# A new order of turns for a gated recurrence and its MLP on one core

## The chip, the core and the metric

The kernel runs on one core of a Trainium2 chip. The metric is the device time of one execution in microseconds (us); it is measured in several runs, and the median is given. A separate execution is recorded by the hardware profiler; from it come the profile page and the trace, a record of every instruction with its start and duration, of the semaphores, and of the single packets that the DMA queues move.

The engines have short names here as in the profile: PE is TensorE (matmul), PEld its weight loads, DVE VectorE, ACT ScalarE, POOL GpSimd, SP SyncE, which issues nearly all transfers. L765 is line 765 of the kernel.

## What is computed

Four sequences (batch b) of 768 steps, 8 heads of 48 channels. A gated linear recurrence runs along each head, and its outputs, joined to rows of 384, go through a layer norm and an MLP of width 1536:

```python
for t in range(S):                                   # S = 768
    state = alpha[:, :, t, :, None] * state + einsum('bhd,bhe->bhde', k[:, :, t], v[:, :, t])
    y[:, :, t] = einsum('bhd,bhde->bhe', q[:, :, t], state)
x = y.transpose(0, 2, 1, 3).reshape(B, S, H * D)     # 4 x 768 x 384
mu, var = mean(x), mean((x - mu) ** 2)               # along each row
xn = (x - mu) / sqrt(var + 1e-06) * g_ln
out = x + maximum(xn @ w_ch1, 0.0) @ w_ch2           # 384 -> 1536 -> 384
```

The two weight matrices come as 8-byte floats; all else is fp32.

## The kernel before, in words

**Chunks.** The 768 steps are cut into six chunks c of 128. The recurrence of one chunk and one sequence is done with matmuls: within a chunk the products of the gates are taken by logarithms, a triangular matmul (L284, L288: `lps`) and exponentials; q and k are scaled by them (L294, L296), transposed on TensorE (L321: `tps`), multiplied with each other (L337, L345: `aps`), masked (L350, L355), and multiplied with v (L397, L407: `yps`) beside the state that comes in. The new state is k times v (L371: `ups`) with the gates (L380 to L386). The gates of a chunk's end go through DRAM (`row`, L301, and `gate`, L361), to turn rows into columns. Chunk 0 takes 128 steps whole, the others as two halves of 64. The result x is stored to DRAM (`kept`, L426), normalized and transposed (L446: `xps`) into `xT`.

**The MLP.** Chunk 0 takes the two products plainly: L476 is xn times w_ch1 (`hps`), L488 the hidden layer times w_ch2 (`ops`). For chunks 1 to 5 all four sequences are done together by a fast matrix scheme: blocks of x and of the weights are added and subtracted first (`combine_x`, `combine_first`, `combine_hidden`, `combine_weights`), then 15 block products per pair of column blocks (L765) and 20 block products (L588) are taken, and each is added into its results by VectorE, ScalarE and GpSimd (L771 to L808, L598 to L648).

**Transfers.** Inputs of a chunk come by SyncE for two sequences at a time: alpha, k, q (`ra`, `rk`, `rq`, L128; later chunks one sequence at a time, L159), v (`vn`, L134, and half of it again with halves swapped, `vx`, L144). The weights come in 12 pieces of 768 KB (`ws`, L192), six of w_ch1 first, into three staging buffers; VectorE and ScalarE turn each into fp32 (L204 to L214), and the end of one lets the load of the third next start. x comes back from DRAM as the start of the result (`ob`, L463) and the results leave by L467.

**What sets the order.** Each part of the work is a Python generator that emits a few instructions and yields. The string `ORDER` (L25) names, letter by letter, whose turn is next, and the loop at L848 takes one step of that generator:

```python
turns = {"YZ"[h]: first_of_chunk_0(h) for h in range(2)}
turns |= {"PQ"[h]: second_of_chunk_0(h) for h in range(2)}
turns |= {chr(ord("a") + n): attention(n // B, n % B) for n in range(NCB * B)}
turns |= {chr(ord("A") + i): take_weights(i) for i in range(len(pieces))}
...
    for turn in ORDER:
        next(turns[turn], None)
```

So a to x are the recurrence of the 24 pairs of chunk and sequence, A to L the weight pieces, Y and Z the first product of chunk 0, P and Q its second, S and W the combined weights, X and N the combined blocks of x and of the hidden layer, M the block products of chunks 1 to 5, V the first block products of the last chunk, R the ReLUs, O the loads of `ob`. No scheduler moves anything afterwards: every engine's queue, SyncE's too, holds its instructions in the order of the string, and a waiting instruction holds up all behind it on its engine. Buffers rotate in the same order: eight PSUM banks, eleven of `sum` and so on. A letter whose generator has ended does nothing.

Of the kernel before, what the change touches and what calls it, by code (L numbers as in the profile page):

```python
# [22 lines left out]


ORDER = (  # L25
    "aaaabbaaddaacbbbbccccaaababbbccdddaaabbbbfeaAfffeeeadaaebbfdaaddceadcccceeeehAdd"
    "gdAccaachbeAgbfbbffffghddddbcggghccibceeeaggghaeebbifffggfBdddddfjcifggeeecAeeCB"
    "hccefiifhhhhcBBYYYdjhiffcjcdYiiYjjZffZiiYYDjDCBDflCCZZZDkYZZZlhhlihhgiiigjjjilYY"
    "gjgghEYYlGEZZGZhEZYlmkhkjggjghllYYYCkkkGEZhlFFHkkiiiYOOFFFlYYenZZZmlhjjYfHHggDjj"
    "GlmjjkeZZZZYhhhSJZYnkkkleekkkkiOlZnkiemmllYZZiinmmmnnfmmYIeIfholHPPSSomjjSSSkSSm"  # L30
    "KIIkkjKKpjJJnnknQfflQoojLLngggmLWWWQPPSPPSSPPpoSoEnhmmgghhnXQXXOXppQppiiiXXQQSSS"
    "mmmnliOjjXXXSmmlnniijMSoWWWoMMrXMMXooMMMMMMmnnnMMMMMRMMmMmMMqMppMMMMMppWMqolorrp"
    "lpppQjjpRRRMMMMMMMpprppMqqqrLnooqqppqqWWWoMMMMRmrMtRMoMMMMRMMMMMMMnnnMMOMMOssqqO"
    "tqsqskMoRooqqtttqWWRNNNMMMMMRRqtNMNNNnnnnNMMMMMMMMMMMlllMkkkMMMkRNNlNNMMNBtvmWtt"
    "pMMNtrllmMMMMrkkrNNMMMMMMMMMossXXXMMtrvvrrrqqqrrXXXooXMMMMMMMXXMMMoXMXrooMMMMMoM"
    "MsMIMMMMsMrMvssvMMMMvtruuustMssrrrtsssuqmMttMMMMRMMMMtMMtuurrrrMMrMppMMMMMMMqROR"
    "MRRRMMMMRRROMpMMMpNOONNNnMMnMMMMRRRNMMMMMNNNMNMMwNMNMMMMMMMMMMMNNNvvMNNvppovxMoM"
    "MMMmMsMMMxqqqvtAXXsssXXvvvXMXvXvttMuMMMMMXXsXuMMMMMMMMMMMuMMMMRMMOtuXMMxMMMMttMM"
    "MMwwwwuquusvuuMMMMMwwwwMMMxuRMMRRRxMMMMMwMRMMRMMMMMMxxxxMMMOOxRMwswwwvRwxuxNNswx"
    "xxNNKquMMMvvttsuuxMMsMMMtRRNNNMMMRMMMxqNNxNwxrrMMMCMMMNMMMONMMNssMMMNMMMMMMvvvww"  # L40
    "vNNMMMwwtXXXXxXxxXMLuuXXMMMXXMMMMMMMMMMMMMMMMMMwMOuMMwxOxxMMvXuuwMMRMMMMMMMMMMMw"
    "JJMMwMMMMMMRRRMMMMMuMRMMMMMvxRRRMMMRMMMMXXXXVXXXOMMXXXRMMRNMMMMMVVNNVVVVVVVNXNMV"
    "VVVRVVVVVMVVVVVVVVVVNRRMNNVVVVVVVVVVVVMRRRRMMMMMVVVVONNNNNMMMMMMNVRVVVVVMMMMMMVV"
    "VRRVVVVRNRNVVOMMNNMMMNGNNMMMMMMNNMMOOKMMMMMMMMMMMNNNRMMMMMMNNNOMMMMHNMMNMMMMMNMM"
    "MMMMMMMM"
)


# [830 lines left out]
```

## Time and profile before

| | |
|---|---|
| median of 3 runs | 437.04 us (436.31 to 439.61) |
| span of the profiled execution | 437.4 us |
| PE busy | 425.6 us, 97%, 4760 rows |
| PEld busy | 379.7 us, 87%, 4760 rows |
| DVE busy | 342.7 us, 78% |
| ACT busy | 202.4 us, 46% |
| POOL busy | 155.3 us, 36% |
| moved by DMA | 45.52 MB, 104 GB/s in the mean |

The profiler gives no time of its execution other than the span, from the first instruction of the kernel to its last. Shares are of the span. "Busy" of TensorE counts overlapping rows once; its matmuls are pipelined, so the distance from one start to the next tells more than the duration of a row. A wait is shown with the engine and line that ended it, by the semaphore that came last; "issue" is a wait for which the profile shows no semaphore. Transfers are counted by queue: queue 1 holds SyncE's, the queues called "instruction" bring the program itself to the engines.

### The profile page before, as it was taken

To read this page: it belongs to the slowest core of one execution; us is meant where nothing else is said; L and a number is where in the kernel's file an instruction comes from. 1 tells how busy PE (TensorE), PEld (TensorE's weight loads), DVE (VectorE), ACT (ScalarE), POOL (GpSimd) and SP (SyncE) were. 2 spreads that over 40 slices of the span, in tenths; PEclk is the share of its full clock that TensorE was granted. 3 is DMA by queue.
4 is the path that set the end of the run, shared out by engine and by line. 5 is a ranking of instruction groups with operands and counts; after the bars stand their busy time and mean duration, and the time that the engine had idled before them with its cause. 6 is when DMAs were issued, how large, how long until landed. Compare 5 with 4: busy or idle time off the path is not lost.

```text
span 437.4 us, 11604 instructions
## 1 busy us (share of the span) xinstructions
PE 425.6 (97%) x4760; PEld 379.7 (87%) x4760; DVE 342.7 (78%) x654; ACT 202.4 (46%) x499; POOL 155.3 (36%) x164
## 2 busy tenths in 40 slices
PE   7996999999999999999999999999999999999996
PEld 5886888875668889998889998889998899999996
DVE  3997899899899789957778776678676579886783
ACT  5694656743535655634274151665256452312000
POOL 1011041220015644052845152663035571628313
PEclk9999999999999999999999999999999999999999
DMA  8979888755063076023342013300033000001201
GB/s 273 325 200 296 272 228 240 186 164 146 37 184 72 21 206 175 6 84 83 58 131 69 18 39 126 59 20 3 1 109 108 1 1 2 0 0 55 90 20 54
DMA packets 54972, 45.52 MB, mean 104 GB/s; under 512 B 26204, under 2 KB 51036, under 8 KB 54920
## 3 DMA queue, kind: packets, MB, share of 16 engines
q1 hardware_dynamic: 54376, 44.63, 34.8%
q8 instruction: 37, 0.61, 0.6%
q10 hardware_dynamic: 544, 0.17, 0.2%
q14 instruction: 15, 0.12, 0.1%
HBM read 35.25 MB, written 9.53 MB: 102 GB/s over the span
## 4 chain that ended last, share of the span: by engine, by line
PE 79%; DVE 9%; DMA 6%; ACT 4%; issue 1%; POOL 0%; SPq 0%; POOLq 0%; DVEq 0%; ACTq 0%
PE ops L588 30%; PE hps L765 29%; PE ops L488 5%; DMA ws<-in_moe_w_ch_dram 3%; PE yps L407 3%; PE aps L345 3%; PE tps L321 2%; PE xps L446 2%; PE hps L476 2%; DVE w L206 2%; PE ups L371 1%; DMA ra<-in_alpha_dram 1%; DMA gate<-row 1%; DVE ws L212 1%; DVE ws L208 1%
## 5 line engine op out<-in xcount | busy, mean ns | idle before, releaser
L604 POOL TENSOR_TENSOR ob<-ob,u 128x192 f32<-128x192 f32 x40 | 25.9, 658 | 81.0 <-DVE ob L601 61.6
L765 PE MATMUL hps<-sum,w 128*128 128x256 f32 x192 | 47.2, 379 | 0.0
L588 PE MATMUL ops<-w,hT 128*128 128x192 f32 x224 | 40.4, 327 | 0.0
L765 PEld LDWEIGHTS hps<-sum,w 128*128 128x128 f32 x192 | 35.9, 190 | 4.6
L386 POOL TENSOR_TENSOR mid<-mid,gate 112x192 f32<-112x192 f32 x20 | 14.6, 732 | 69.0 <-DVE mid L384 55.3
L816 ACT ACTIVATE hT<-hT 128x512 f32<-128x512 f32 x48 | 28.1, 630 | 21.6 <-POOL hT L787 13.2
L588 PEld LDWEIGHTS ops<-w,hT 128*128 128x128 f32 x224 | 37.1, 190 | 0.5
L476 PE MATMUL hps<-xT,w 128*128 128x256 f32 x144 | 32.6, 380 | 2.9 <-DVE qk L294 2.9
L765 PE MATMUL hps<-xT,w 128*128 128x256 f32 x136 | 34.6, 381 | 0.0
L476 PEld LDWEIGHTS hps<-xT,w 128*128 128x128 f32 x144 | 26.7, 190 | 6.4 <-issue 3.0
L488 PE MATMUL ops<-w,hT 128*128 128x384 f32 x96 | 31.7, 487 | 0.0
L588 PE MATMUL ops<-ws,sum 128*128 128x192 f32 x160 | 28.8, 326 | 0.0
L488 PEld LDWEIGHTS ops<-w,hT 128*128 128x128 f32 x96 | 17.9, 190 | 11.9 <-ACT qT L328 0.2
L765 PEld LDWEIGHTS hps<-xT,w 128*128 128x128 f32 x136 | 25.3, 190 | 3.3
L588 PEld LDWEIGHTS ops<-ws,sum 128*128 128x128 f32 x160 | 26.3, 190 | 0.0
L386 POOL TENSOR_TENSOR st<-st,gate 112x192 f32<-112x192 f32 x16 | 12.9, 808 | 36.4 <-DVE st L384 36.4
L598 DVE TENSOR_TENSOR ob<-ops,ob 128x192 f32<-128x192 f32 x50 | 17.0, 350 | 11.1 <-PE ops L588 5.3
L321 PE MATMUL tps<-consts,qk 128*112 128x128 f32 x176 | 24.2, 275 | 0.6 <-DVE qk L296 0.6
L345 PE MATMUL aps<-qT,kT 48*64 48x64 f32 x640 | 23.3, 222 | 0.7 <-issue 0.7
L588 PE MATMUL ops<-ws,hT 128*128 128x192 f32 x128 | 23.4, 326 | 0.0
L321 PEld LDWEIGHTS tps<-consts,qk 128*112 128x112 f32 x176 | 19.9, 134 | 3.7 <-DVE qk L296 1.3
L784 POOL TENSOR_TENSOR hT<-hT,u 128x512 f32<-128x512 f32 x8 | 10.2, 1275 | 34.6 <-DVE u L783 34.5
(230 smaller groups left out, 1175.2 us busy)
## 6 DMA issues: line engine op xcount, KB each, us to landing
ws<-in_moe_w_ch_dram SPq DMA_DIRECT2D x12, 768.0 KB
vn<-in_v_dram SPq DMA_DIRECT2D x12, 384.0 KB
kept<-x SPq DMA_DIRECT2D x24, 192.0 KB
ob<-kept SPq DMA_DIRECT2D x24, 192.0 KB
out_dram<-ob SPq DMA_DIRECT2D x19, 192.0 KB
ra<-in_alpha_dram SPq DMA_DIRECT2D x16, 192.0 KB
rk<-in_k_dram SPq DMA_DIRECT2D x6, 384.0 KB
rq<-in_q_dram SPq DMA_DIRECT2D x6, 384.0 KB
```

Source lines behind the costliest of these rows:

```text
L321: nc.tensor.transpose(tps[:, p], qk_of(c, b)[:, i, p].rearrange("p a b -> p (a b)")[:, :R], ident)
L345: nc.tensor.matmul(aps[0][halves[1 - i], p, s], kT[rs, p, s], qT[rs, p, s], start=True, stop=True)
L386: nc.gpsimd.tensor_mul(new, new, by)
L407: nc.tensor.matmul(yps[r][halves[s], i, p], of, by, start=True, stop=True)
L476: nc.tensor.matmul(hps, w1[:, j // 2, f, j % 2 * P:][:, :P], xT_of[0][:, f, bs], start=(f == 0), stop=(f == NF - 1))
L488: nc.tensor.matmul(ops_of[b], hT_of[c][:, j, b], w2[:, j], start=(j == 0), stop=(j == NJ - 1))
L588: nc.tensor.matmul(acc, lhs[:, j], rhs[:, j], start=(j == 0), stop=(j == NT - 1))
L598: nc.vector.tensor_add(x, acc, x)
L604: getattr(nc.gpsimd, f"tensor_{op}")(x, x, y)
L765: nc.tensor.matmul(acc[:, i], w, b, start=True, stop=True)
L784: add_late(c4, c4, u2)
L816: nc.scalar.activation(out=x, in_=x, func=AFT.Relu)
```

## The change

Only the string is replaced, by one with the same steps of the same generators in another sequence; functions, buffers, instructions and transfers are as before. The new string is one row shorter, so every later line of the changed file has a number lower by one. The start and the end of both:

```diff
 ORDER = (
-    "aaaabbaaddaacbbbbccccaaababbbccdddaaabbbbfeaAfffeeeadaaebbfdaaddceadcccceeeehAdd"
-    "gdAccaachbeAgbfbbffffghddddbcggghccibceeeaggghaeebbifffggfBdddddfjcifggeeecAeeCB"
-    "hccefiifhhhhcBBYYYdjhiffcjcdYiiYjjZffZiiYYDjDCBDflCCZZZDkYZZZlhhlihhgiiigjjjilYY"
-    "gjgghEYYlGEZZGZhEZYlmkhkjggjghllYYYCkkkGEZhlFFHkkiiiYOOFFFlYYenZZZmlhjjYfHHggDjj"
...
-    "VRRVVVVRNRNVVOMMNNMMMNGNNMMMMMMNNMMOOKMMMMMMMMMMMNNNRMMMMMMNNNOMMMMHNMMNMMMMMNMM"
-    "MMMMMMMM"
+    "aabbabcaadbadaaabbdcacabcdbabcbabcfdafaceabbaAdecddecbefbeceadcbedcebffeAbechdcg"
+    "ahbAgdcebadfcfgafAfgdbfbdghccadgdfhabcafgegefagbhBAeidfgececigfacChhdjihffdfihei"
+    "icegeBdefffihciYiBdjBYhcYdYgYjdYjYcjjZjiZYhlZgeZhlBCDihCZjZDfZCegYZYZYghgjZhCYik"
+    "hZEiiDjEDZkgjklgjgElZYhZkglFYFEgkYjYhGlZliYlhHmkZZllhZFkiYYGkmeHljjkYknjhimlSZlY"
...
+    "NVRMMMVVMVNMVVMMNVVVVMVRORNMMVNVNVVVVVVVVRVVVVMMMMMVRVVNMVNMVMVOMRMMMMMNMMVNMVVV"
+    "VRRMRMVMVMNRMVVMONONNMRMNMVMMMNOVMNMMNMNMMNRMMMMMNMMMMMMNMNMMMNMMNMMNMMMMMMM"
 )
```

The old string is 1528 letters long, the new 1516. In the old one 716 letters equal the one before them, in the new one 292: the turns of one generator are more often spread among others.

More of the change, by code (lines that the diff above doesn't have):

```diff
@@ L25 @@
 ORDER = (
-    "aaaabbaaddaacbbbbccccaaababbbccdddaaabbbbfeaAfffeeeadaaebbfdaaddceadcccceeeehAdd"
-    "gdAccaachbeAgbfbbffffghddddbcggghccibceeeaggghaeebbifffggfBdddddfjcifggeeecAeeCB"
-    "hccefiifhhhhcBBYYYdjhiffcjcdYiiYjjZffZiiYYDjDCBDflCCZZZDkYZZZlhhlihhgiiigjjjilYY"
-    "gjgghEYYlGEZZGZhEZYlmkhkjggjghllYYYCkkkGEZhlFFHkkiiiYOOFFFlYYenZZZmlhjjYfHHggDjj"
-    "GlmjjkeZZZZYhhhSJZYnkkkleekkkkiOlZnkiemmllYZZiinmmmnnfmmYIeIfholHPPSSomjjSSSkSSm"
-    "KIIkkjKKpjJJnnknQfflQoojLLngggmLWWWQPPSPPSSPPpoSoEnhmmgghhnXQXXOXppQppiiiXXQQSSS"
@@ L32 @@
[L32 to L43, printed above, removed]
@@ L44 @@
-    "VRRVVVVRNRNVVOMMNNMMMNGNNMMMMMMNNMMOOKMMMMMMMMMMMNNNRMMMMMMNNNOMMMMHNMMNMMMMMNMM"
-    "MMMMMMMM"
+    "aabbabcaadbadaaabbdcacabcdbabcbabcfdafaceabbaAdecddecbefbeceadcbedcebffeAbechdcg"
+    "ahbAgdcebadfcfgafAfgdbfbdghccadgdfhabcafgegefagbhBAeidfgececigfacChhdjihffdfihei"
+    "icegeBdefffihciYiBdjBYhcYdYgYjdYjYcjjZjiZYhlZgeZhlBCDihCZjZDfZCegYZYZYghgjZhCYik"
+    "hZEiiDjEDZkgjklgjgElZYhZkglFYFEgkYjYhGlZliYlhHmkZZllhZFkiYYGkmeHljjkYknjhimlSZlY"
+    "iGljnZfkFHZelmkmYnGlnjImPkmYZllSYSJikSmoiISPhZmeImkIQZSioSOkmnJhkomiQefoigHjJojk"
@@ new lines @@
+    "hjfkfhnPknjOeSLKfSQLnkPmKKoLSPgighgefgiPShpWSognoQmpnSmWXpOnSXlXnWPmQmopnpXQmoQW"
+    "XXWlpWnnXilmkMXjSmXWMMMSlMnOnMnMXMSlMmjMMrMPMMMOjnXMroMMMQprMkjMnMMMMMMWronOMMRM"
+    "ppWMpMqMMrMqpoMqRpoppnpMproRMMMRqMqOMoqMMRRMMikLMMjMompjMMqMkptMMmMolsMiqRqqMpRt"
+    "kOMqpqsRqptqnNWsoMtMWsMMMRpNNMRWMlpNMMlMMNsMMRNNmnNNMMNMMqMtMrtkMoMMlNNMMNtOvMrM"
+    "tMMNrNqMWlqrNsMqMoMMMMOMkXMMXXqvrXXMMXXXrMMMMrMtuMtXXMqMMMvMXMMMMMMqruMtvsuMsMpM"
+    "MstMpMMtrsRMMMMtMsMuRoMMOvMpORMMrMRMMrrMRMnMMoMMMsMMMsmMMtMtMrsMRRMRMvMRotMqMMNR"
@@ new lines @@
+    "mMsqMNMqMNRoMNMMMNMNMNNJumrMRnMMsNMxMMNNopMMoMuMMpsMMuMmMNOnNuNMMMMMNNvrMMvMMMMv"
+    "MorqMvMsMXMxtvOMsnxXvtXtvvXMXuMXXrMXsrMXMMvwXMMMvMMsrsMMuMMXMMMMstMMqMRwuRuuOvuM"
+    "MxORwvMsMxMRwMMxMMMxwwMsMMMMMtMRssMMMMMuRtMxvMtxtMuwMRxwMMMwuwxMRxwxwxwwxMMRrMxM"
+    "uRMwMMwMRMMMxMNwNNNxvMqMNxtMMRMNNrMNMMMMMMxMwurNNsMNtqMMNMwMtMNMXNMMMXNNXXMXMMwv"
+    "MMXMMuwMXvMwMMMXxwMMMMMXxMXMMMMMMMMXMMMMMvMMMMMRuMMMMxMxRwuMMMMRMRMMuuxMMMMMMMMM"
+    "MMMRMwMMMvROuvxMMMRMOMMMvuMwOXRXXXXXVXXMRXMNRMRNVNNMKMMXVMVVVVNVVNMVVVVRMVVXVVVM"
```

## The prediction

> **What bounds the kernel now.** I read first the busy table and the slices of the page, then TensorE's waits, then the timeline of TensorE around each wait, then the DMA queues.
>
> ```profile
> PE 425.6 (97%) x4760; PEld 379.7 (87%) x4760; DVE 342.7 (78%) x654; ACT 202.4 (46%) x499; POOL 155.3 (36%) x164
> ...
> PEclk9999999999999999999999999999999999999999
> DMA  8979888755063076023342013300033000001201
> ...
> q8 instruction: 37, 0.61, 0.6%
> ...
> PE 79%; DVE 9%; DMA 6%; ACT 4%; issue 1%; POOL 0%; SPq 0%; POOLq 0%; DVEq 0%; ACTq 0%
> ```
>
> TensorE is busy nearly all the time at full granted clock, and 79% of the chain is TensorE. Its rows stand at a fixed pitch: 216 ns from start to start for L765 and L476, 162.5 for L588, 323 for L488, 109 for the transposes L321 and L446. An fp32 matmul makes two such rows and a transpose one: 2,512 matmuls, 264 of them transposes, are the 4,760 rows. So a reordering can win only what TensorE loses between rows, and can lose by making TensorE's work itself dearer or by new waits.
>
> The small matmuls of the recurrence (L288, L337, L345, L371, L397, L407) come in islands between the full-size ones. The timeline of one island:
>
> ```profile
> 74.63 0.38 PE L476 MATMUL hps<-xT,w 128*128 128x256 f32 x1
> 74.94 0.54 PE L288 MATMUL lps<-la,consts 64*64 64x384 f32 x2
> ...
> 75.94 0.67 PE L371 MATMUL ups<-vn,qk 64*48 64x48 f32 x30
> 76.54 0.65 PE L321 MATMUL tps<-consts,qk 128*112 128x128 f32 x4
> ```
>
> The last L476 row starts at 74.63 and the island at 74.94: 0.31 us where the pitch is 0.216, so going in costs 0.09. From the last L371 row (76.39) to the transpose are 0.15: coming out costs that. Both numbers repeat at nearly every island; switches among full-size lines (L765 to L588, L588 to L321 and back) cost 0.00. Inside, I fitted the undisturbed islands: L288 with its L345 0.99 us, 16 L371 0.46, 32 L407 0.93 (counts are the program's matmuls). Summing all rows in the order of the program gives **416.5 us of TensorE work**; the span has 437.4, so 20.9 is lost: 3.6 at the end after the last matmul, the rest in waits.
>
> ```profile
> PE hps L476 <- DVE qk L294: 2.9, 1, 2.9
> PE ups L371 <- issue: 1.2, 2, 0.8
> ...
> 36.27 1.46 PE L476 MATMUL hps<-xT,w 128*128 128x256 f32 x6
> 40.58 0.81 PE L476 MATMUL hps<-xT,w 128*128 128x256 f32 x3 [2.85 <-DVE qk L294]
> ...
> 217.45 0.60 PE L371 MATMUL ups<-vn,qk 64*64 64x48 f32 x27 [0.84 <-issue]
> ```
>
> The largest wait is put down to VectorE's L294, but in the program that matmul waits for a VectorE instruction done at 35.7. Counting TensorE's rows (weight loads, matmuls and semaphore waits), the stalls at 32.4 (0.9 us longer than the pitch), 37.4 (3.2), 84.7 (0.6) and 216.4 (1.0) stand at counts 961, 1217, 2753 and 6081: differences 256, 6x256 and 13x256. Queue 8, "instruction", moved 37 packets, of 16 KB each in the packet records, for 9,600 rows. So these are waits for a block of 256 instructions. In all four TensorE resumes 2.4 to 2.7 us after a q8 packet starts (30.74, 37.92, 82.87, 215.07). **Together they cost 5.7 us.**
>
> When is the packet late? After a stall the request is made as TensorE enters the block: entered 33.29, next packet 37.92; 40.58, 44.40; 85.34, 86.97; 217.45, 218.48. Late by 4.6, 3.8, 1.6 and 1.0 us. The long ones fall where the kernel's transfers are saturated:
>
> ```profile
> 33.30:37.40 4.10, 4.10 (x127) 3.92 (x128) 2.09 (x7) 2.55 (x9) 1.52 (x3) 1.00 0.85 278
> 37.40:40.60 3.20, 0.35 (x3) 0.16 (x2) 3.13 (x6) 1.98 (x4) 0.51 (x1) 1.00 1.12 307
> ```
>
> (columns: stretch, length, busy time of TensorE, weight load, VectorE, ScalarE, GpSimd, granted clock, DMA share, GB/s.) The bytes fit a queue: 1,152 KB were issued and not moved at 33.29 (a 768 KB weight piece, 384 KB of v), and the packet comes when about that much has flowed. The page "DMA: Bandwidth & Descriptors" of the Trainium skill, under "Queues, rings and completion order", says that an engine alternates between queues at packet boundaries; by that the block would start within about a packet, and the order of the transfers would not matter to it. The 4.6 us at full DMA load against 1.0 to 1.6 at part load speak against it here, and I go by the rows.
>
> **The change, part by part.** Instruction and transfer counts are equal; the work is reordered on every queue.
>
> *TensorE's own work.* The same groups make 29 islands instead of 21. Eight more times in and out at 0.09 + 0.15 are **+1.9 us** (418.5). Ends: 0 if islands overlap with waits (three or four of the eight lie before 45 us, where TensorE waits anyhow), +2.9 if every L288 that follows L371 or L407 inside an island (ten against one) adds the 0.1 that one added in the island at 164.5. I take 1.9.
>
> *Blocks in the middle.* A block lasts as long as its instructions take. Before, four blocks last under 2 us (ending at counts 2753, 4545, 6081, 6849); two of them stalled, for 0.6 and 1.0, two did not, where the block begins right behind full-size matmuls and so is asked for early. After, one is left (ending at 8129, 2.0 us, only L407, and it begins one matmul before its island); the next shortest past count 1473 have 4.5 to 5.6 us. So **-1.6 us**, and for the one left +0.4, between 0 and 1.0.
>
> *Blocks in the front.* The block to 961 takes 3.96 us of work instead of 4.39, the one to 1217 3.31 instead of 4.03: they hide less. The two weight pieces that before are SyncE's 40th and 47th transfer stand 40th and 41st, so at the request for block 1217 up to 1,536 KB are queued instead of 1,152: at the 300 to 330 KB/us of these stretches the packet starts near 38.4 and the block is there near 41.1. Before, TensorE passed this point at 40.58 with 29.8 us of work done; now at 41.1 with 29.2: **+1.1 us**. Ends: -4.4 if the queue is empty then (packet 1.0 after the request), +3.5 if the next piece and the next v (1,152 KB) are in front too. The trace has no such order; 4.6 us of queueing is the nearest row.
>
> *Semaphore waits.* Those of before after 41 us are 0.4 at 55.4 (L355), 0.3 at 101.3, 0.2 at 201.2 and 0.6 at 335.6 (the L446 behind L440). Following each wait in the program back to TensorE with the durations of the rows, the least distance to spare past the first 10 us of work is 0.2 us in both orders, and the 5th percentile is 1.1 us after and 0.95 before; VectorE's work due by 50 to 120 us of TensorE's work is 3 to 5 us less, later equal. So no new wait is in sight; half of the old 1.5 go: **-0.7**. Ends -1.5, +2 (VectorE is 90% busy from 10 to 183 us, so one step in a bad place makes others late). SyncE's issues in the first 20 us of work are the same but for k and q of the second pair, now ahead of the first gate row: 0, between -0.7 and +0.7. ScalarE's and GpSimd's cumulative work stays tens of microseconds ahead of need past 100 us: 0. The tail holds the same last products, stores and 3.6 us: 0.
>
> Sum on the profiled execution: 437.4 + 1.9 - 1.6 + 0.4 + 1.1 - 0.7 = 438.5. The page gives no time for that execution beyond its span, which lies 0.4 above the median of the runs, 437.04. So **438.1 us**. Within 1% (432.7 to 441.4) is about what a measurement tells from no change.
>
> If the whole front stall is longer than about 3.4 us, the page "TensorE: Matmul & The Clock Gate", under "HAM oscillation", expects the clock to fall to half for a window of that length, an estimated 1.7 us more; the 3.2 us stall at 37.4 left the granted clock at 1.00, and no row here has a longer one past the start.
>
> **Rivals.** (1) *Slower: transfers in front of block 1217.* If the third weight piece and v are issued before TensorE enters that block, 3.5 us are added: 442. For it: the pieces are issued back to back. Against: v must wait for an L407 group that comes at 28 us of work. It decides from a q8 packet that starts past 41 us. (2) *Faster: the front stalls go.* If the request finds an empty queue, 4.1 of the 4.4 us go, the 0.9 at 961 too, and the other 0.7 of semaphore waits perhaps: 433. For it: only two transfers differ. Against: 33 to 47 us is saturated before. (3) *It does nothing of the kind:* the stalls move to the blocks of 4.5 to 5.6 us behind stores and loads, some 1.6 in all: 440.
>
> **How the numbers follow.** Forecast 0.53, rival 1 0.23, rival 2 0.18 (two thirds of it beyond 1%), rival 3 0.06. Faster by over 1%: 0.12; slower: 0.23; within: 0.65. The range reaches to the middle of rivals 1 and 2: 433.0 to 443.0.
>
> **What would show it.** Right: islands 29, TensorE's work 418.5; no wait "issue" at L371 past 50 us; q8 packets near 31 and 38.4 and a wait of 4 us near 37. Wrong: no wait there (rival 2), one of 7 us (rival 1), or long waits of TensorE for VectorE or a store, which I expect nowhere.

## The result, and the profile after

The changed kernel takes **441.82 us** (median of 11 runs, 439.59 to 443.36), the kernel before 437.51 us beside it (11 runs, 436.31 to 439.61): ratio **1.0084, 95% interval 1.0060 to 1.0107**. It is 4.3 us slower, by 0.84%; forecast was 1.1 us slower. The profiled executions have spans of 437.4 and 441.6 us, 4.2 apart, so the two traces show the difference that is to be explained.

The page of the changed kernel (busy table, two rows of the slices, queue 8, the chain of work that ended last):

```profile
PE 431.4 (98%) x4760; PEld 382.8 (87%) x4760; DVE 337.4 (76%) x654; ACT 200.6 (45%) x499; POOL 152.0 (34%) x164
...
PEclk9998899999999999999999999999999999999999
DMA  8988466776315561133320033220015000001201
...
q8 instruction: 37, 0.61, 0.5%
...
PE 95%; ACT 2%; issue 1%; DMA 1%; DVE 0%; SPq 0%; DVEq 0%
```

TensorE's share of the chain went up from 79% to 95%, and yet the kernel is slower. The share is no count of TensorE's waits: up to 95 us the chain of before ran largely through transfers and VectorE, that of after mostly through TensorE. The row PEclk, all nines before, has two eights in its fourth and fifth slice, 33 to 55 us. TensorE's waits say what is left, and where:

```profile
PE yps L406 <- issue: 3.4, 1, 3.4
PE lps L283 <- ACT la L277: 2.0, 2, 1.4
...
PE ups L370 <- issue: 0.3, 1, 0.3
```

(The line numbers are one lower than before.) One wait of 3.4 us with no semaphore behind it, one of 0.3, and past 45 us none at all (one of 0.2 at an L445 ends at 32.99). Before, the waits past that point came to 3.1 us. The timeline of TensorE around the long one:

```profile
42.17 0.34 PE L406 MATMUL yps<-vn,at 64*64 64x48 f32 x2 [3.43 <-issue]
43.85 1.10 PE L320 MATMUL tps<-consts,qk 128*112 128x128 f32 x4
44.74 2.77 PE L475 MATMUL hps<-xT,w 128*128 128x256 f32 x6
```

Six L475 rows take 2.77 us; the six of the kernel before, at full clock, took 1.46. The stretches (length, busy time of TensorE, weight load, VectorE, ScalarE, GpSimd, granted clock, DMA share, GB/s):

```profile
35.20:38.50 3.30, 3.30 (x124) 3.06 (x127) 2.67 (x8) 2.84 (x10) 1.95 (x4) 1.00 0.93 339
38.50:41.10 2.60, 0.24 (x17) 0.12 (x9) 2.53 (x4) 1.24 (x6) 0.32 (x1) 1.00 1.06 365
41.10:44.50 3.40, 2.33 (x60) 2.24 (x60) 0.03 (x1) 0.50 (x2) 0.00 (x0) 0.51 1.06 373
44.50:48.00 3.50, 3.50 (x13) 2.79 (x11) 2.81 (x6) 2.33 (x4) 0.00 (x0) 0.50 1.05 325
48.00:55.00 7.00, 7.00 (x68) 6.12 (x67) 3.64 (x9) 2.01 (x5) 0.00 (x0) 1.00 0.18 12
```

TensorE stands from 38.52 to 42.17, and the clock is at half from 41.14 to 47.97, 6.83 us. TensorE worked 5.8 us of that at half speed and lost some 2.8.

**Where the 4.2 us are.** For each trace I take, at a point of the program, the time less the TensorE work done by then (the same sum of rows as in the prediction). What it grows by is what TensorE lost:

| at us of work | before | after | difference |
|---|---|---|---|
| 20 | 5.65 | 7.51 | +1.9 |
| 27.5 | 7.67 | 9.24 | +1.6 |
| 34 | 10.79 | 15.77 | +5.0 |
| 60 | 11.41 | 16.13 | +4.7 |
| 200 | 14.01 | 17.51 | +3.5 |
| last full-size group | 17.28 | 19.79 | +2.5 |
| work in all | 416.5 | 418.5 | +2.0 |

**The first 34 us of work cost 5.0 us more; all that comes later 0.5 less** (2.5 less lost, 2.0 of work added); the tail is 0.3 shorter. Of the 5.0, 1.9 are lost by 20 us of work and some 2.8 in the half clock. The experiments take the front apart.

Blocks of instructions: TensorE enters the blocks that end at counts 961 and 1217 at 29.69 and 35.18, the packets of queue 8 come 2.91 and 4.49 us later (32.61 and 39.67), and TensorE goes on 2.6 and 2.5 us after that, having stood 0.48 and 3.65 us. Before, these stalls had 0.94 and 3.23. Their sum is unchanged, 4.13 against 4.17.

### The profile page after: what moved, and what is told of

Read it like the earlier page. It is cut to its first block, busy times and chain, and to the rows that moved or that the text cites. A ratio compares the mean times of both kernels' runs of the same rounds, so it can differ in the third digit from the quotient of the medians.

```text
span 441.6 us, 11610 instructions
## 1 busy us (share of the span) xinstructions
PE 431.4 (98%) x4760; PEld 382.8 (87%) x4760; DVE 337.4 (76%) x654; ACT 200.6 (45%) x499; POOL 152.0 (34%) x164
## 4 chain that ended last, share of the span: by engine, by line
PE 95%; ACT 2%; issue 1%; DMA 1%; DVE 0%; SPq 0%; DVEq 0%
PE hps L764 30%; PE ops L587 30%; PE hps L475 8%; PE ops L487 7%; PE yps L406 5%; PE tps L320 5%; PE aps L344 4%; PE ups L370 3%; PE xps L445 2%; PE lps L287 1%; PE lps L283 1%; PE aps L336 1%; DMA ra<-in_alpha_dram 1%; PE yps L396 0%; ACT la L277 0%
## 5 line engine op out<-in xcount | busy, mean ns | idle before, releaser
L603 POOL TENSOR_TENSOR ob<-ob,u 128x192 f32<-128x192 f32 x40 | 27.2, 691 | 75.5 <-DVE ob L600 62.5
L385 POOL TENSOR_TENSOR mid<-mid,gate 112x192 f32<-112x192 f32 x20 | 13.0, 650 | 94.5 <-DVE mid L383 63.7
L815 ACT ACTIVATE hT<-hT 128x512 f32<-128x512 f32 x48 | 29.0, 630 | 24.8 <-POOL hT L786 13.7
L475 PE MATMUL hps<-xT,w 128*128 128x256 f32 x144 | 35.1, 393 | 0.0
L764 PE MATMUL hps<-xT,w 128*128 128x256 f32 x136 | 35.0, 381 | 0.0
L487 PE MATMUL ops<-w,hT 128*128 128x384 f32 x96 | 32.9, 490 | 0.0
L475 PEld LDWEIGHTS hps<-xT,w 128*128 128x128 f32 x144 | 27.2, 196 | 3.7
L320 PE MATMUL tps<-consts,qk 128*112 128x128 f32 x176 | 26.5, 280 | 0.0
L406 PE MATMUL yps<-vn,at 64*64 64x48 f32 x320 | 22.2, 224 | 3.4 <-issue 3.4
L320 PEld LDWEIGHTS tps<-consts,qk 128*112 128x112 f32 x176 | 21.2, 137 | 4.2 <-issue 1.0
L344 PE MATMUL aps<-qT,kT 48*64 48x64 f32 x640 | 24.3, 221 | 0.0
L406 PEld LDWEIGHTS yps<-st,qT 48*64 48x64 f32 x320 | 20.9, 138 | 3.0 <-issue 1.6
```

The source lines that it names most:

```text
L320: nc.tensor.transpose(tps[:, p], qk_of(c, b)[:, i, p].rearrange("p a b -> p (a b)")[:, :R], ident)
L344: nc.tensor.matmul(aps[0][halves[1 - i], p, s], kT[rs, p, s], qT[rs, p, s], start=True, stop=True)
L385: nc.gpsimd.tensor_mul(new, new, by)
L406: nc.tensor.matmul(yps[r][halves[s], i, p], of, by, start=True, stop=True)
L475: nc.tensor.matmul(hps, w1[:, j // 2, f, j % 2 * P:][:, :P], xT_of[0][:, f, bs], start=(f == 0), stop=(f == NF - 1))
L487: nc.tensor.matmul(ops_of[b], hT_of[c][:, j, b], w2[:, j], start=(j == 0), stop=(j == NJ - 1))
```

## The experiments

OLD and NEW stand for the two strings; "rest of" a string is that string without the steps that have been taken. Every ratio is to the kernel before on the same chip.

| | ratio, 95% interval | profiled span | its clock | front stalls |
|---|---|---|---|---|
| after | 1.0084 [1.0060, 1.0107] | 441.6 | 0.991 | 0.48, 3.65 |
| e1 old front | 0.9958 [0.9928, 0.9987] | 434.6 | 1.000 | 0.82, 2.13 |
| e2 new front | 1.0195 [1.0152, 1.0237] | 446.1 | 0.989 | 3.3 |
| e3 blocks shifted | 1.0109 [1.0063, 1.0155] | 441.2 | 1.000 | 3.18 |
| e4 20 switches | 1.0172 [1.0106, 1.0237] | 445.3 | 1.000 | 0.82, 2.40 |
| e5 old first 60 | 1.0040 [1.0011, 1.0068] | 437.8 | 0.996 | 2.99 |
| e6 piece apart | 1.0076 [1.0047, 1.0105] | 440.9 | 0.991 | 0.21, 3.37 |
| e7 768 KB ahead | 1.0019 [0.9997, 1.0040] | 437.0 | 1.000 | 0.86, 2.13 |
| e8 = e1 again | 0.9984 [0.9958, 1.0010] | 436.3 | 0.996 | 0.32, 2.68 |
| e9 768 KB behind | 0.9964 [0.9941, 0.9987] | 435.8 | 0.995 | 2.44 |
| e10 front shifted | 0.9982 [0.9961, 1.0003] | 434.0 | 1.000 | none |
| e11 shifted in the warm-up | 0.9977 [0.9957, 0.9997] | 436.2 | 1.000 | 0.28, 0.74 |
| e12 before, shifted | 1.0011 [0.9991, 1.0031] | 437.0 | 0.999 | none |

### e1_old_front: is the loss in the front?

```diff
-ORDER = NEW
+ORDER = OLD[:280] + (rest of NEW)
```

> The first 280 letters of the old order (about 52 us of TensorE's work), then the remaining steps in the new order: 25 islands, 417.5 us of TensorE's work. Theory (the loss of the new order is made in its first 48 us: later loads, a block stall of 3.65 us and a stretch of half clock behind it; its later part is better than the old one by 2.6 us of waits, less 1.0 of work): span about 435.8 us, granted clock 1.00, a block stall near 37 us as before. Rival A (the loss is spread: island switches and waits all along): about 439.5 us. Rival B (the later part is the worse one): 441 us or more.

Measured: 437.07 us against 439.0, 0.9958. The old front with the new later part is faster than either whole order in this comparison. TensorE around the front stall, and beyond it:

```profile
35.55 1.46 PE L476 MATMUL hps<-xT,w 128*128 128x256 f32 x6
38.77 1.46 PE L476 MATMUL hps<-xT,w 128*128 128x256 f32 x6 [1.75 <-DVE qk L294]
```

The stall is 2.13 us (label and size of the bracket are the profile's; the block count is 1217), and the six rows behind it take 1.46 us: full clock. At 34 us of work the loss stands at 8.98 (before 10.79, after 15.77), and from there to the end it grows by 4.29 (before 6.49, after 4.02). So the loss of the change is in the front, and its later part is a gain of some 2 us less the islands. The fronts of e1 and of the kernel before are the same instruction for instruction, so the 1.8 us between 8.98 and 10.79 are a difference of executions; the 5 to 7 us to the changed kernel are well beyond it.

### e2_new_front: the front alone

```diff
-ORDER = OLD
+ORDER = NEW[:280] + (rest of OLD)
```

> The first 280 letters of the new order, then the remaining steps in the old one: 25 islands, 417.5 us of work. Theory: span about 443.2 us, granted clock near 0.99, block stall of 3.6 us near 38.5 us and block stalls at L371 later as in the old order. Rival A: about 439.5 us. Rival B: 437 us or less.

Measured: 447.73 us, 1.0195, in the direction expected and 3 us beyond it. TensorE's waits name two places at the seam of the two strings that neither whole order has:

```profile
PE yps L407 <- issue: 3.0, 1, 3.0
...
PE ups L371 <- DVE w L206: 2.1, 1, 2.1
...
PE ups L371 <- DVE x L417: 0.7, 1, 0.7
```

The first is the front stall. The others, at 89.1 and 76.9 us, are TensorE waiting for VectorE, 2.8 us together, and behind the longer one the clock is at half again, from 91.5 to 94.9. That is where the excess is; the run confirms the front, but its size only after the seam is taken off.

### e3_shift_blocks: same order, the block boundaries elsewhere

52 small matmuls on zeros, used by nothing, behind the third L283 (here L284); each has four instructions, so all later boundaries lie 208 earlier in the work.

```diff
             nc.tensor.matmul(lps[:, :DM], tri, a, start=True, stop=True)
+            for i in range(52 if b == 2 else 0):
+                nc.tensor.matmul(idle[halves[i % 2], :48], zero[halves[i % 2], :64],
+                                 zero[halves[i % 2], :48], start=True, stop=True)
```

> The new order with 52 small matmuls on zeros more at the start, behind the third L284, while TensorE waits there; they only move every block boundary by 208 instructions (that is, to places 48 instructions later in the work). Theory (the stall is the instruction block behind two weight pieces): the stalls of 0.5 and 3.65 us at 34.7 and 38.5 go from their matmuls; the boundaries now fall about 1.5 us of work later, one stall of about 2.8 us near 39.5 stays, below the length that brings the clock down: clock 1.00 and span about 437.5 us. Rival (the matmul at 38.5 waits for data, and the count of instructions is chance): the same wait at the same matmul, clock 0.99, 441.6 us or up to 1.5 more.

Measured: 443.54 us, 1.0109, expected 437.5. The stalls did move as they should. None is left at the matmuls where they were (35.18 and 42.17 of the changed kernel), and one stands at the new boundary, count 1473:

```profile
44.83 0.20 PE L410 MATMUL yps<-mid,qT 48*64 48x48 f32 x1 [2.96 <-issue]
```

3.18 us from start to start, where 2.8 was expected. Matmul by matmul against the changed kernel, this one is 3.20 us late from the fillers on (12.4 us), 2.7 late at 37.9, 0.9 early after the place of the old stall, 2.1 late after its own, 0.15 early at 47.5, when the changed kernel has got through its half clock, and 0.4 early from 50 on. So 3.2 us were paid for the fillers and the total says nothing; the boundaries say that the stalls belong to the blocks and not to the matmuls or to what these read.

### e4_20_switches: the price of one island

The old order with one 64x64 matmul by 48 columns ahead of each of the 20 products L588 (here L590) of the last chunk. What it writes is overwritten by the product.

```diff
+        if c + 1 == NCB:
+            nc.tensor.matmul(acc[:64, :48], lhs[:64, 0, :64], rhs[:64, 0, :48], start=True, stop=True)
         for j in range(NT):
             nc.tensor.matmul(acc, lhs[:, j], rhs[:, j], start=(j == 0), stop=(j == NT - 1))
```

> The old order, with one 64x64x48 matmul in front of each of the 20 block products of the last chunk, into the bank that the product then overwrites. Theory (0.09 us into and 0.15 out of the small shape, and 0.03 for the matmul): 20 x 0.27 = 5.4 us more, span near 442.8, and 0.27 more from start to start at each. Rival (a switch hides behind the queued weight loads, and what was read as its cost is the small matmuls' own): 20 x 0.03 = 0.6 us more, 438.0.

Measured: 446.81 us, 1.0172, some 7.6 us for 20 switches. The timeline of one:

```profile
405.64 1.46 PE L590 MATMUL ops<-w,hT 128*128 128x192 f32 x8
407.03 0.31 PE L588 MATMUL ops<-w,at 64*64 64x48 f32 x2
407.27 1.57 PE L590 MATMUL ops<-w,at 128*128 128x192 f32 x8
408.77 0.31 PE L588 MATMUL ops<-ws,qk 64*64 64x48 f32 x2
```

Eight L590 rows at the pitch of 162.5 ns end 1.30 us after 405.64; the small row starts 93 ns later. Its two rows take 93.5 and 148.5 ns from start to start, and then comes what I had not counted: from 407.27 to the next small row are 1.50 us, 0.093 for the next way in and 0.10 more than eight pitches. The first full-size row behind an island takes 267 ns instead of 162.5 (0.06 more where a transpose comes first, in the islands of the kernel). A switch in and out costs **0.345 us**, not 0.24. With the 93.5 ns of its first row, each of the 20 takes 0.44 us more, 8.8 together; the span is only 7.9 longer because the front stalls of this execution are 0.95 shorter (0.82 and 2.40 against 0.94 and 3.23).

### e5_old_first_60: only the first loads and first steps

```diff
-ORDER = NEW
+ORDER = OLD[:60] + (rest of NEW)
```

> The first 60 letters of the old order (the first 20 transfers, 15 us of TensorE's work), then the remaining steps in the new one; the two weight pieces stay back to back. Theory (about 1.5 of the 4.7 us that the new front costs come from the first 20 us, where k and q of the second pair go ahead of the first gate row and one L284 later): TensorE reaches 20 us of work 1.5 us sooner than in the new order, then the same long block stall and half clock: span about 440 us, clock 0.99. Rival (the front of the new order is late only by the stall and the clock behind it): 441.6, no sooner.

Measured: 439.80 us, 1.0040. At 20 us of work TensorE has lost 6.3 us instead of 7.5, 1.1 to 1.2 us of the 1.9 by which the change is late there. Later:

```profile
39.33 0.26 PE L407 MATMUL yps<-vn,at 64*64 64x48 f32 x2 [2.77 <-issue]
40.80 1.10 PE L321 MATMUL tps<-consts,qk 128*112 128x128 f32 x4
41.69 2.17 PE L476 MATMUL hps<-xT,w 128*128 128x256 f32 x6
...
45.75 1.46 PE L476 MATMUL hps<-xT,w 128*128 128x256 f32 x6
```

The stall is 2.99 us, and only the first rows behind it are slow: the clock is at half from 39.7 to 43.1, one window instead of two. In these two profiles 3.8 us of span come back for sixty turns: 1.2 early, 1.1 of the two stalls (0.48 and 3.65 against 2.99), the rest clock. The profiled execution of the changed kernel is the slowest of its 11 runs, though; by the ratios, 1.0040 against 1.0084, it is 1.9 us.

What is it in the first turns? ScalarE and TensorE at the start of the changed kernel, from the timeline:

```profile
7.92 0.49 ACT L291 ACTIVATE lps<-lps 128x384 f32<-128x384 f32 x1
...
8.32 0.51 ACT L277 ACTIVATE la<-ra 128x384 f32<-128x384 f32 x1
...
8.88 0.91 PE L283 MATMUL lps<-la,consts 128*128 128x384 f32 x2 [1.39 <-ACT la L277]
...
11.11 0.53 ACT L277 ACTIVATE la<-ra 128x384 f32<-128x384 f32 x1
...
11.69 0.91 PE L283 MATMUL lps<-la,consts 128*128 128x384 f32 x2 [0.58 <-ACT la L277]
```

and in e5, which has them as before:

```profile
6.74 0.51 ACT L278 ACTIVATE la<-ra 128x384 f32<-128x384 f32 x1
...
7.30 0.91 PE L284 MATMUL lps<-la,consts 128*128 128x384 f32 x2 [0.75 <-ACT la L278]
...
7.93 0.51 ACT L278 ACTIVATE la<-ra 128x384 f32<-128x384 f32 x1
...
8.50 0.91 PE L284 MATMUL lps<-la,consts 128*128 128x384 f32 x2 [0.28 <-ACT la L278]
```

ScalarE takes the logarithms of the third and fourth sequence (L277) behind the exponentials of the first two and more, at 8.32 and 11.11 us instead of 6.74 and 7.93, and the gate products that wait for them come 1.6 and 3.2 us later. Its first logarithm is late too, 4.33 us instead of 3.70.

### e6_piece_apart: does the load beside the block make it late?

The fourth weight piece is issued 20 turns later, nothing else.

```diff
-    "...gegefagbhBAeidfgececigfacChhdjihffdfihei"
+    "...gegefagbhBeidfgececigfacChhdjiAhffdfihei"
```

> The new order with one letter moved: the load of the fourth weight piece, 20 turns later, so that v and x go between it and the second piece. Theory (the block of count 1217 waits for the bytes ahead of it): some 0.3 MB less are in front of its request, so the packet comes 0.5 to 1 us sooner, the stall falls from 3.65 to about 2.9, and the half clock goes: span 438 us, clock 1.00 or 0.996. Rival (blocks do not wait for the kernel's bytes): stall 3.65, 441.6 us.

Measured: 440.99 us, 1.0076. The block's packet comes at 38.92 instead of 39.67, but TensorE had entered the block 0.38 earlier, so that the packet came 4.12 us after the request instead of 4.49. The stall is 3.37, not the 2.9 expected, and the two windows of half clock stay:

```profile
41.51 0.34 PE L407 MATMUL yps<-vn,at 64*64 64x48 f32 x2 [3.16 <-issue]
...
44.09 2.76 PE L476 MATMUL hps<-xT,w 128*128 128x256 f32 x6
```

The distance of the two pieces, which my front term was built on, is worth about 0.4 us.

### e7_768KB_more and e9_768KB_behind: what must flow before the block

Both are e1 with one more copy of 768 KB from DRAM to DRAM, used by nothing: in e7 ahead of the second weight piece as 16 large packets, in e9 behind it in rows of 1.5 KB.

```diff
         dst, src = pieces[i]
+        if i == 1:                                   # e7
+            junk = dram.tile([512, DM], FP32, name="junk", tag="junk", bufs=1)
+            nc.sync.dma_start(junk, v[0, :512].rearrange("s h d -> s (h d)"))
...
         nc.sync.dma_start(dst, src)
+        if i == 1:                                   # e9
+            junk = dram.tile([512, 512], FP32, name="junk", tag="junk", bufs=1)
+            nc.sync.dma_start(junk[:, :DM], v[0, :512].rearrange("s h d -> s (h d)"))
```

> The kernel of e1_old_front with 768 KB more, copied from DRAM to DRAM, issued right ahead of the second weight piece; the copy is used by nothing. Theory: the block of count 1217 comes later by the time of those bytes, 2.0 to 2.5 us, so the stall grows from 2.1 to 4 us or more, and two windows of half clock follow: span about 439.5 us, clock 0.99. Rival (blocks take turns with the transfers packet by packet): stall within 0.3 us of before, 434.6 us plus what late weights cost, at most 1.

> The kernel of e1_old_front with 768 KB more, copied from DRAM to DRAM in rows of 1.5 KB like those of the inputs, issued right behind the second weight piece and ahead of v; the copy is used by nothing. Theory F (the block waits for all bytes issued ahead of its request): packet 2 us later after its request, 5.9 us instead of 3.9, stall at count 1217 of 4 us or more, half clock behind it, span 438.5 us or more. Theory L (while the queues are full a block takes about 4 us to start, whatever stands ahead): 3.6 to 4.6 us from request to packet, stall 2.0 to 2.9, span 434 to 436 us plus what late v or weights cost.

Measured: e7 438.62 us, 1.0019; e9 436.51 us, 0.9964. In e7 the packet of block 1217 comes 3.85 us after the request (e1: 3.89), the stall is 2.13 in both; the copy costs something else, a new wait of 1.0 us at 44.6, the last of these lines (the first is the front stall); the second weight piece comes later there, and I read the wait as its consequence:

```profile
PE hps L479 <- issue: 1.8, 1, 1.8
...
PE hps L479 <- ACT qT L331: 1.0, 1, 1.0
```

The copy flowed beside the waiting block: its 16 packets start between 33.18 and 34.35 us and end between 35.46 and 36.18, and the request is at 33.35. In e9 the copy was queued behind the piece at the request: packet after 4.27 us, stall 2.44. Counted as bytes issued less bytes moved, some 2,050 KB were outstanding at the request in both, against 1,390 in e1. At 300 to 400 KB/us a block that waits for all queued bytes would have come some 2 us later. It came at the same time in e7 and 0.4 later in e9, when 1,256 and 1,509 KB had moved. So at this load the delay does not count the bytes ahead:

| block | us to the packet | KB moved by queue 1 meanwhile | stall |
|---|---|---|---|
| before, 1217 | 4.63 | 1,265 | 3.23 |
| after, 1217 | 4.49 | 1,528 | 3.65 |
| e1 | 3.89 | 1,234 | 2.13 |
| e7 | 3.85 | 1,256 | 2.13 |
| e9 | 4.27 | 1,509 | 2.44 |
| e6 | 4.12 | 1,292 | 3.37 |
| e10, 1473 (about the same place in the work) | 3.38 | 1,158 | 0 |
| e10, 961, transfers at part load | 0.65 | 214 | 0.02 |

(The number is the count at which the block ends. A packet of e7 that flows over an edge of the stretch is counted by its share.) While the transfers are saturated a block takes 3.4 to 4.8 us to its packet, whichever of these loads stand in front, and 2.2 to 2.7 more until TensorE goes on. Some 6.5 us less the block's own work is the stall. What sets the 4 us stays open.

With less outstanding the delay does go with the bytes. For the blocks that end at 961, 1217 and 1473 in all 14 traces, it is 0.65 to 2.4 us where 430 to 820 KB were outstanding as TensorE entered, 2.1 to 3.3 us at 930 to 1,200 KB, and 3.4 to 4.8 us (one block 2.7) from 1,300 to 2,300 KB, without growing there: e1 has 3.89 us at 1,390 KB, the changed kernel 4.49 at 2,040, e6 4.15 at 2,310. (Where no stall stands at the start of a block, its request may have gone out earlier than this.)

The page "DMA: Bandwidth & Descriptors" of the Trainium skill ("Queues, rings and completion order") lets each engine alternate between queues at packet boundaries. That bytes beyond some 1,300 KB do not add to the delay agrees with it; that the packet is 3.4 to 4.8 us late under load, and 0.65 at part load, is more than one packet of another queue, and no run here shows why.

### e8_old_front_again: the same kernel, with and without a window of half clock

```diff
 (e1, unchanged)
```

> The kernel of e1_old_front once more, for a narrower interval: 0.995 of the kernel before (0.993 to 0.998).

Measured: 438.13 us, 0.9984. The profiled execution of e1 had a stall of 2.13 us and full clock; this one 2.68, and then:

```profile
34.00:38.80 4.80, 2.70 (x37) 2.33 (x30) 4.22 (x10) 3.63 (x9) 1.38 (x3) 1.00 1.10 335
38.80:42.20 3.40, 3.20 (x9) 2.28 (x8) 2.56 (x4) 0.37 (x2) 0.00 (x0) 0.50 1.03 360
42.20:47.00 4.80, 4.80 (x117) 4.47 (x117) 2.08 (x5) 2.02 (x5) 0.00 (x0) 1.00 0.75 277
```

Half clock from 38.8 to 42.2. Matmul by matmul it is 0.23 us behind e1 at the end of the stall and 1.79 behind after the window, and the spans are 1.8 apart. That is one window's price on one kernel, 1.6 us, and it is what separates executions of the same program. e1 beat the kernel before in the first comparison and not in the second: the gain of the hybrid order is at most a few tenths of a per cent.

### e10_front_shifted: the front stalls taken away

e1 with 29 small matmuls behind the second and the fourth L284: boundaries 232 earlier, where blocks of 4.2 to 7 us of work begin.

```diff
+            for i in range(29 if b in (1, 2) else 0):
+                nc.tensor.matmul(idle[halves[i % 2], :48], zero[halves[i % 2], :64],
+                                 zero[halves[i % 2], :48], start=True, stop=True)
```

> The kernel of e1_old_front with two times 29 small matmuls on zeros at the start, behind the second and the fourth L284, where TensorE waits for ScalarE; they move every block boundary by 232 instructions, so that the three blocks from 22 us of work on last 4.2, 5.8 and 7.1 us of work instead of 4.4, 4.0 and 6.9. Theory L (stall = 4 us to the packet + 2.5 us to the block - work of the block before): stalls of 0.8 and 2.1 become 1.0 and 0.4, no window of half clock: 1.5 us less than e1_old_front in the span, less up to 1 us that the small matmuls may cost at the start; 0.992 of the kernel before. Rival (the stalls are where data arrive): the same 2.1 us wait at the same matmul, ratio 0.997 to 1.000.

Measured: 437.01 us, 0.9982, the time of e1. The front stalls are gone, none is over 0.1 us, and TensorE is busy without a break at full clock:

```profile
30.00:36.00 6.00, 6.00 (x215) 5.69 (x213) 5.81 (x14) 5.16 (x18) 1.97 (x3) 1.00 0.81 203
36.00:42.00 6.00, 6.00 (x124) 5.34 (x122) 5.60 (x12) 3.95 (x10) 1.01 (x2) 1.00 1.07 329
```

The gain was spent at the start:

```profile
5.88 1.95 PE L286 MATMUL lps<-more 64*64 64x48 f32 x58
...
9.24 1.95 PE L286 MATMUL lps<-more 64*64 64x48 f32 x58
11.12 1.09 PE L324 MATMUL tps<-consts,qk 128*112 128x128 f32 x8
```

Two rows of fillers of 1.95 us each (L286), and the first transpose at 11.12 us instead of 9.20 in e1. Against e1 it is 1.9 late there, 1.2 late at 33, 0.8 early at 38.8 and 0.5 early from 40.5 to the end. Stalls of 2.7 us were won, 1.9 were paid.

### e11_shift_for_nothing and e12_before_shifted: the same shift, without the fillers?

The eight products on zeros that begin the program (L231) are replaced by 66 small ones, so that the shift of 232 needs no filler later: in e11 on e1, in e12 on the whole old order.

```diff
-    for _ in range(8):
-        nc.tensor.matmul(idle[:, :P], zero, zero, start=True, stop=True)
+    warm = [slice(64 * s, 64 * s + 64) for s in range(2)]
+    for i in range(66):
+        nc.tensor.matmul(idle[warm[i % 2], :48], zero[warm[i % 2], :64],
+                         zero[warm[i % 2], :48], start=True, stop=True)
```

> The order of e1 (first 280 turns old, the rest new). Instead of small matmuls added behind the second and fourth L284, the eight 128x128 products on zeros with which the program starts (L231, 1.05 to 4.6 us, before any data have come) are replaced by 66 small ones (64x64 by 48, on the same zeros, used by nothing): 58 matmuls more, so every block boundary stands 232 instructions earlier in the work, as in e10, but without the 1.9 us that TensorE was later in e10 at its first transpose. Theory (the stalls are the block's delay less the block's work, and e10 was no faster than e1 only because its fillers stood in TensorE's way): no stall over 0.2 us between 25 and 50 us, granted clock 1.00, first transpose at 9.2 as in e1, span 434.0 - 1.9 = 432.1, ratio to before about 0.989. Rival G (time won at the stalls is given back later, to VectorE or to transfers that come no sooner): stalls gone, but span 434 to 435, ratio about 0.995. Rival H (small products do not raise the clock as the large ones do): the granted clock is 0.50 for one window more after 4.6 us, and the first transpose comes 1 to 2 us later; ratio 0.995 or more.

> The kernel before, whole old order, with the same 66 small matmuls in place of the eight of L231, so that its block boundaries stand 232 instructions earlier. Theory: the stalls of 0.9 and 3.2 us in the front go (at most 0.3 left), and with them the half clock that follows in some runs; in the middle six blocks of 1.9 to 2.4 us of work arise instead of four of 1.9 to 2.0, of which two stalled for 0.6 and 1.0: 1 to 3 us there instead of 1.6. Span 437.4 - 4.1 + 0.5 = 433.8, ratio about 0.990. Rival G (given back): ratio 0.995 to 1.0. If the blocks in the middle stall for more than 1 us each, 5 us there: ratio 1.0.

Measured: e11 437.97 us, 0.9977; e12 439.20 us, 1.0011. Both missed. The warm-up did not come free, as e11 shows:

```profile
1.05 6.41 PE L232 MATMUL lps<-more 64*64 64x48 f32 x132 [1.05 <-DVE more L228]
```

It lasts 6.41 us, where e1's eight large products are through by 4.63. Up to 6.2 us each small matmul takes 107 ns, behind that 58 ns; the profile's record of the granted clock begins, at full, at 6.28. So most of them ran at half speed, which the fillers of e10 (58 in 3.9 us, with the clock at full from 4.27) did not. The first gate product comes 2.76 us later than in e1. Then e11 wins 0.9 and 1.9 us at the two front boundaries, loses 0.6 and 1.1 around its own (0.28 and 0.74 of them stalls), and ends 1.6 behind. This is neither rival G nor H as written (the clock came to full at 4.27 to 7.00 us in the kernels with the large products, so 6.28 is not late), but the fillers' price once more.

e12 is 2.0 us late at its first transpose, 2.1 early at 38.4 when both front stalls are gone, and then loses it to the middle, where its boundaries meet short blocks:

```profile
PE ups L373 <- issue: 2.1, 2, 1.1
```

These are two waits that end at 84.76 and 217.09 us, 1.3 us each from start to start, in place of the two of 0.6 and 1.0 in the kernel before. At the end the span is 437.0 against 437.4. What a shift takes from one block it gives to another; the new order's later part is what keeps e10 and e11 ahead of e12.

**The clock over all runs.** Of e10, e11 and e12, whose front has no stall over 0.74 us, none of 36 runs has a mean clock below 0.998. Of the kernel before, with its 3.2 us stall, 37 of 92 runs have 0.995 to 0.996, which is one window of 3.4 us. Of the changed kernel one run of 11 has 1.000, five have one window and five two (0.991 to 0.992). A window is worth 1.6 us in e8 and about 2 in the runs, so 1.4 windows a run against 0.4 make some 2 us of the 4.3 between the medians.

**What decides whether half clock follows.** In all 14 profiles the granted clock changes only at whole multiples of 3.413 us from where its record begins. I cut each span into these windows and take the share of each in which TensorE had a row. Of 1,767 windows at full clock 21 had a share of 0.40 or less (14 of them at the end of the program), and half clock followed each of them; it followed none of the 1,746 with 0.42 or more. Of 10 windows at half clock, the three with 0.70 to 0.73 were followed by another, the seven with 0.93 or more by full clock. So it is not the length of a stall that counts but how much of it falls into one window, and where the windows lie differs from one execution to the next:

| execution, its stall | window | TensorE's share | next window |
|---|---|---|---|
| e5, 2.99 | 36.29 to 39.70 | 0.19 | half |
| after, 3.65 | 37.72 to 41.14 | 0.30 | half |
| e8, 2.68 | 35.36 to 38.78 | 0.39 | half |
| e9, 2.44 | 35.20 to 38.62 | 0.40 | half |
| before, 3.23 | 38.71 to 42.13 | 0.45 | full |
| e1, 2.13 | 36.21 to 39.62 | 0.49 | full |
| e3, 3.18 | 39.82 to 43.23, 43.23 to 46.65 | 0.60, 0.53 | full |

The stalls of before and of e3 are cut in two by an edge of a window; that of e8, shorter than both, lies nearly whole in one.

## Why the prediction was right and where it was wrong

The direction, the class (within 1%) and the range held; the size did not: +1.1 us forecast, +4.3 measured, and nearly all of the miss is the front: +1.1 forecast there, 5.0 measured in the profiles. The term that gave the forecast its direction, the blocks in the front, measured about nothing; the slowdown came from the start and the clock, which the sum had at 0 or not at all. So the direction held partly by luck, and the range too: its upper part stood for rival 1, which did not happen.

- **Behind the front, right.** Forecast +1.9 for islands, -1.6 and +0.4 for blocks, -0.7 for semaphores: 0.0 together. Measured -0.5. In detail: 29 islands and 418.5 us of work as counted. Each new island cost 0.345 us by e4, not 0.24, since the first full-size row behind it is slower too: 2.4 to 2.8 us, not 1.9. No stall for a block past 45 us, so the two of 0.6 and 1.0 went as forecast; the one short block left did not stall (0 instead of +0.4). All of the semaphore waits went, 1.5 instead of 0.7. The errors cancel.
- **"SyncE's issues ... 0, between -0.7 and +0.7": wrong.** The first sixty turns alone cost 1.1 to 1.2 us (e5), outside that range. But it is not SyncE that I should have followed: ScalarE takes the logarithms L277 of the third and fourth sequence later, and TensorE's waits for them went from 1.0 to 2.0 us, as the timeline in e5 shows. I had weighed only the transfers of these turns, and of the waits only those past the first 10 us of work, where everything has an operand to spare; the chain from L277 by L283 to the first transposes has none.
- **"Blocks in the front, +1.1": right in the place, wrong in cause and size.** The stalls stand at counts 961 and 1217 as said, at the end of the blocks of 4.0 and 3.3 us of work, and e3 shows by the shift that the boundaries make them. TensorE goes on behind 1217 at 42.17 with 2.2 us more lost than before; forecast was 41.1 and 1.1. But the stalls have no part in that: together they lasted 4.13 us against 4.17 (3.0 to 4.2 in the profiles with the old front, before, e1, e4 and e8; 3.3 to 4.1 with the new, after, e2 and e6). Nearly all of the 2.2 is the 1.9 of the start, which delayed the request too: packets at 32.61 and 39.67 where I had them near 31 and 38.4. The reading of a queue of 1,536 KB instead of 1,152 falls with e7 and e9: at this load bytes ahead do not add, and the delay was 4.49 us against 4.63 although more was outstanding, some 2,040 KB against 1,310. What made the long stall longer was the other half of that paragraph, 3.3 us of work in the block instead of 4.0; the other stall got shorter by about as much, 0.46 against 0.42 us. (The 300 to 330 KB/us of that term are high: the two stretches shown have 278 and 307 GB/s.)
- **The clock was left out of the sum: the largest single term.** "The 3.2 us stall at 37.4 left the granted clock at 1.00" was true of one execution, and I took it for the rule of the kernel. The profile of the changed kernel loses 2.8 us by half clock. The page "TensorE: Matmul & The Clock Gate" ("HAM oscillation") has the clock fall to half when TensorE idles for more than some 3.4 us. The forecast stall of "4 us" was past that bound, so its 1.7 us belonged in the sum. The bound does not fit the runs, though: windows follow stalls of 2.28 (e2, at 91.4 us), 2.44, 2.68 and 2.99 us here, and none came after 2.40 in e4's profile, 3.18 in e3's or 3.23 before. What fits all of them is the share of one window, 0.40 or less. Judged by that, the 3.2 us stall of before said nothing for the next execution.
- **The rivals.** Rival 1 names nearly the measured time, 442, by a mechanism that did not happen: no packet past 41, no stall of 7 us. Rival 2 and 3 did not occur: the front stall stayed, and no stall for a block came back later.
- **The span and the median.** Executions for which both are on record are 1.7 to 1.9 us longer in device time than in span, in every run. Before's profiled execution was thus near 439.2, at the slow end of its runs, and not 0.4 from the median. It does no harm, since only the difference of 1.1 was carried to the median.

What stays open: what makes a block wait about 4 us under load, and the 0.7 us of the early loss that lie outside the first sixty turns.

## What to carry to other kernels

A stall that looks like a semaphore wait but stands at a fixed number of the engine's instructions is its program arriving late. It is shortened by giving the block that ends there more work, or by fewer transfers in flight when the block before it begins (here, only below some 1,300 KB); instructions added to shift it cost what they take, and the shift hands the stall to another block. Price a TensorE stall of more than about 2.3 us with the half clock that may follow, 1.6 us or more for a window: an estimate from the shares above is that 2.05 us without a row in one window of 3.41 bring it, so that a stall of 2.3 to 4 us brings it or not by where it falls, and a longer one always. Look at several executions before saying that it doesn't come. When an order is searched anew, follow every engine's first 10 us by hand: what is put ahead of the first operands there costs nearly its whole time, since nothing lies beside it yet.

## What the runs showed of the hardware that was not expected

- A row of full size right behind 64x64 matmuls takes 104 ns more than its pitch of 162.5, beside 93 ns on the way in (e4).
- 64x64 matmuls by 48 columns as the first work of the program take 107 ns each up to 6.2 us and 58 ns behind that, where the record of the granted clock begins at full (e11: 66 in 6.41 us).
- Half clock comes in whole windows of 3.41 us on a grid whose place differs between executions. It follows a window in which TensorE had rows for 0.40 of the time or less (21 of 21), and no other window at full clock (0 of 1,746); so the same program has it in one execution and not in the next (e1 and e8).
- Under saturated transfers the packet of an instruction block starts 3.4 to 4.8 us after its request, and 768 KB more in front of it did not lengthen that beyond this spread (e7, e9); below some 1,300 KB outstanding the delay falls, to 0.65 us.
